# First MLP layer of token blocks 0 and 1 by seven products of halves for four of the seven chunk pairs, with the folded weights stored instead of kept in a buffer

## The chip, the core and the metric

The kernel runs on one core of one Trainium2 chip. A core has TensorE (PE), which multiplies matrices into PSUM banks; VectorE (DVE), ScalarE (ACT) and GpSimd (POOL), which do element-wise work; SyncE (SP), which here issues the transfers; and DMA engines, which carry them out. Every engine takes its own instructions in order, and semaphores order the engines against each other. The metric is the device time of one execution in microseconds (us).

## The reference

There are 2048 tokens of 640 features. The input is layernormed to `xn`, and the output is `x + attention(xn) + mlp(xn)`, where the MLP layernorms again:

```
x = A_x
xn = _layernorm(x, axis=-1)
return x + _A_ref(xn, A_wqkv, A_w_phi, A_wo) + _B_ref(xn, B_w1, B_b1, B_w2, B_b2)

# _B_ref: the MLP, 640 -> 1728 -> 640
y = _layernorm(x, axis=-1)
h = _gelu(jnp.einsum("bsd,df->bsf", y, w1) + b1)
return jnp.einsum("bsf,fd->bsd", h, w2) + b2

# _A_ref: linear attention, 32 heads of 20
pq = jnp.einsum("bhsd,hdf->bhsf", q, w_phi)
pk = jnp.einsum("bhsd,hdf->bhsf", k, w_phi)
phi_q = jnp.concatenate([_softmax(pq, axis=-1), _softmax(-pq, axis=-1)], axis=-1)
...
kv = jnp.einsum("bhsf,bhsd->bhfd", phi_k, v)
num = jnp.einsum("bhqf,bhfd->bhqd", phi_q, kv)
```

All operands are float32. `w_phi` follows the projections to q and k with nothing between, so the kernel multiplies it into their weights ahead of time; this product is called a fold.

## The kernel before, in words

**Exact products.** Every float32 operand is split into a high part, rounded to the type that PE takes in one pass (fp32r), and a low part, the rest. A product is then three matmuls, high by high, high by low and low by high (`mm3`, L61 to L64). Splitting is a copy on ACT (`hi`) and a subtraction on DVE or POOL (`lo`; both in `split`, L49 to L59). One group of three matmuls over 512 tokens is called a step below.

**Tiles.** Tokens come in four blocks of 512 (`b`). The 640 features are five k-chunks of 128 (`KC`). The 1728 hidden features are 14 chunks of 128 (the last has 64), worked on as seven pairs `g` = 0 to 6. The blocks 0 and 1 go through the MLP first, from about 18 to 130 us: this is the stage of the change. For a pair and a block, `Mlp.passes` (L258) does the first layer, 2 chunks x 5 k-chunks = 10 steps, with the GELU on ACT after each chunk (L251), and then the second layer, 5 output chunks x 2 = 10 steps, each output added to `acc[b]` by DVE (L300). The first layer of the next block or pair goes ahead of the second layer of the last, so that the GELU has time. PSUM banks 0 to 2 (`ph`) hold first layers, 5 to 7 (`po`) second layers, 3 and 4 (`px`) side work.

**Side work.** After every `mm3` of the first and second layers the generator `mlp.beside` is advanced by one (L247, L293); what it issues lands in the engines' queues at that place. In this stage it is `prep` (L567): the folds (`folds`), seven pairs of banks ten steps apart, products on PE (L510), highs on ACT (L528), lows on DVE (L530); the statistics of the tokens of blocks 2 and 3; then the row pairs: their means and scales are transposed on PE (L186), copied by DVE (L188), stored by SP (L189) and read back spread over all partitions (L193); the weights of v; and the layernormed tokens of blocks 2 and 3, on POOL (L603), DVE (L606), ACT (L610) and DVE (L613), stored for later (L615).

**Folds.** For each group of six heads the fold of k goes straight into the resident tile `wkv_` (wkh, wkl), that of q into a tile `t`, of which there are three, and from it to HBM in two stores (L533); the three narrow columns per head (18 of a group) go into `wkv_` too.

**Order.** PE's order is the order of the program text (L309), and so is that of DVE, ACT and POOL in this stage (L379). SP's order is chosen by a scheduler. A tile of a pool with n buffers waits for the readers of the tile n before it, transfers included.

## Time and profile before

| what | value |
|---|---|
| median of 3 runs | 712.67 us (711.66 to 712.88) |
| profiled execution, its own time | 713.22 us |
| span of its instructions | 711.3 us |
| mean granted TensorE clock | 1.000 |
| PE busy | 705.2 us, 99% of the span |
| DVE, ACT, POOL busy | 486.7, 334.4, 387.1 us |
| transfers | 98.25 MB, 138 GB/s on the mean |

"Busy" counts the time in which an engine has an instruction under way; register, branch and issue instructions don't count. In a list of groups a row has the line, engine, operation, output and inputs with shapes, the count, then busy time and mean nanoseconds of one, then the idle time of the engine ahead of the group and what ended it. In a timeline a row has start and duration in us, with the idle time ahead and its releaser in brackets. In the list of PE's waits a row has us in total, times and the longest. In a table by windows a row has the stretch, its length, busy time of PE, weight loads, DVE, ACT and POOL with counts, the granted clock, the share of the DMA engines and GB/s. PE's matmul rows overlap, since it is pipelined; the distance of their starts is what one costs.

### The profile page before, as it was taken

The numbers are of one execution on the slowest core, as the hardware profiler recorded it, in microseconds if no ns is written. First come the engines' busy times: TensorE is split into PE (matmuls) and PEld (weight loads), VectorE is DVE, ScalarE is ACT, GpSimd is POOL, SyncE is SP. The second block draws the span as 40 slices with busy tenths as digits, with TensorE's granted clock in tenths as the row PEclk, the third lists the DMA queues.
The fourth block names the chain that finished last, engine by engine and source line by source line (L and its number), as shares of the span: only waits on it lengthen the run. The fifth ranks groups of instructions, "written<-read, shape, count | busy, mean of one in ns | idle before, by whom it ended". The sixth has DMA issues, their size and how long they took to land.

```text
span 711.3 us, 9753 instructions
## 1 busy us (share of the span) xinstructions
PE 705.2 (99%) x3392; PEld 596.3 (84%) x3392; DVE 486.7 (68%) x827; ACT 334.4 (47%) x574; POOL 387.1 (54%) x339
## 2 busy tenths in 40 slices
PE   9999999999999999999999999999999999999998
PEld 7888888888888888888888888878888888888886
DVE  7837555875543798798788887745575656778653
ACT  7824355334213563464355458455565556551310
POOL 2011222465103896897787878556587777553400
PEclk9999999999999999999999999999999999999999
DMA  9714675454151313723600705774444653163222
GB/s 331 286 30 130 196 215 188 168 192 163 48 223 75 109 63 152 178 93 148 148 0 1 185 1 189 177 211 124 134 128 124 201 159 105 46 233 122 88 75 88
DMA packets 67924, 98.25 MB, mean 138 GB/s; under 512 B 14788, under 2 KB 37972, under 8 KB 66252
## 3 DMA queue, kind: packets, MB, share of 16 engines
q1 hardware_dynamic: 67876, 97.64, 43.4%
q8 instruction: 26, 0.43, 0.2%
q14 instruction: 22, 0.18, 0.1%
HBM read 67.27 MB, written 30.35 MB: 137 GB/s over the span
## 4 chain that ended last, share of the span: by engine, by line
PE 90%; issue 3%; DMA 2%; POOL 2%; DVE 2%; ACT 0%; SPq 0%; POOLq 0%; ACTq 0%
PE bank L62 27%; PE bank L64 26%; PE bank L63 26%; PE bank L748 2%; DMA r<-in_w 2%; PE bank L510 2%; PE bank L975 1%; PE bank L974 1%; POOL w L56 1%; PE bank L353 1%; PE bank L295 1%; PE bank L296 1%; PE bank L276 1%; PE bank L277 1%; DVE st L128 0%
## 5 line engine op out<-in xcount | busy, mean ns | idle before, releaser
L56 POOL TENSOR_TENSOR w<-r,w 128x640 fp32r<-128x640 f32 x48 | 77.7, 1639 | 111.5 <-ACT w L53 83.9
L62 PE MATMUL bank<-y,w 128*128 128x512 f32 (+1 forms) x310 | 120.3, 388 | 0.0
L64 PE MATMUL bank<-y,w 128*128 128x512 f32 (+1 forms) x310 | 119.9, 387 | 0.0
L63 PE MATMUL bank<-y,w 128*128 128x512 f32 (+1 forms) x310 | 119.8, 386 | 0.0
L62 PE MATMUL bank<-m,w 128*128 128x512 f32 x266 | 105.0, 395 | 0.2 <-DVE acc L300 0.2
L64 PE MATMUL bank<-m,w 128*128 128x512 f32 x266 | 103.6, 390 | 0.0
L63 PE MATMUL bank<-m,w 128*128 128x512 f32 x262 | 102.0, 389 | 0.0
L300 DVE TENSOR_TENSOR acc<-bank,acc 128x512 f32<-128x512 f32 x120 | 81.3, 683 | 27.9 <-PE bank L64 22.2
L62 PE MATMUL bank<-wkh,y 128*128 128x512 f32 (+2 forms) x240 | 87.6, 365 | 0.0
L63 PE MATMUL bank<-wkl,y 128*128 128x512 f32 (+2 forms) x240 | 87.1, 363 | 0.0
L64 PE MATMUL bank<-wkh,y 128*128 128x512 f32 (+2 forms) x240 | 86.9, 362 | 0.0
L64 PEld LDWEIGHTS bank<-y,w 128*128 128x128 f32 x310 | 58.2, 188 | 11.9
L63 PEld LDWEIGHTS bank<-y,w 128*128 128x128 f32 x310 | 58.3, 188 | 11.7
L62 PEld LDWEIGHTS bank<-y,w 128*128 128x128 f32 x310 | 58.2, 188 | 11.6
L713 POOL TENSOR_TENSOR m<-m,mx 128x640 f32<-128x640 f32 (+2 forms) x48 | 44.5, 941 | 42.8 <-DVE mx L701 42.8
L694 ACT ACTIVATE m<-bank 128x512 f32<-128x512 f32 (+1 forms) x64 | 26.5, 440 | 86.0 <-PE bank L64 62.6
L968 POOL TENSOR_TENSOR e<-e,m 128x512 fp32r<-128x512 f32 x28 | 40.0, 1430 | 39.4 <-ACT m L967 35.3
L62 PEld LDWEIGHTS bank<-m,w 128*128 128x128 f32 x266 | 50.0, 188 | 10.7 <-DVE acc L300 0.8
L64 PEld LDWEIGHTS bank<-m,w 128*128 128x128 f32 x266 | 49.9, 188 | 10.5
L720 DVE TENSOR_REDUCE sm<-m 128x64 f32<-128x1280 f32 x32 | 47.3, 1479 | 15.8 <-ACT m L718 15.6
L63 PEld LDWEIGHTS bank<-m,w 128*128 128x128 f32 x262 | 49.2, 188 | 9.6
L251 ACT ACTIVATE m<-bank,b1t 128x512 f32<-128x512 f32 (+1 forms) x54 | 36.2, 671 | 43.8 <-PE bank L64 42.8
(225 smaller groups left out, 1462.7 us busy)
## 6 DMA issues: line engine op xcount, KB each, us to landing
r<-in_w SPq DMA_DIRECT2D x52, 320.0 KB
e<-e SPq DMA_DIRECT2D x40, 256.0 KB
e<-acc SPq DMA_DIRECT2D x52, 160.0 KB
acc<-in_xT SPq DMA_DIRECT2D x4, 1280.0 KB
xb<-in_x SPq DMA_DIRECT2D x8, 320.0 KB
t<-in_x SPq DMA_DIRECT2D x8, 320.0 KB
raw<-in_xT SPq DMA_DIRECT2D x10, 256.0 KB
yh<-t SPq DMA_DIRECT2D x10, 256.0 KB
```

The costliest lines, as they stand in the source:

```text
L56: eng.tensor_tensor(lo, src, f(hi), op=ALU.subtract)
L62: nc.tensor.matmul(ps, lh, rh, start=first, stop=False, **kw)
L63: nc.tensor.matmul(ps, lh, rl, start=False, stop=False, **kw)
L64: nc.tensor.matmul(ps, ll, rh, start=False, stop=last, **kw)
L251: self.last = nc.scalar.activation(gt, pz, AF.Gelu_apprx_tanh, bias=b1t[:, 2 * g + j:2 * g + j + 1]).ins
L300: nc.vector.tensor_tensor(acc[b][:, m, :], pw, acc[b][:, m, :], op=ALU.add)
L510: nc.tensor.matmul(ps[:, c + i * kd:c + (i + 1) * kd], raw[n, g][:, (kc + i) * P:(kc + i + 1) * P], wpt[:, g, :kd // DF, 1:], start=True, ...
L694: return nc.scalar.activation(p3[:, :, c], ps.rearrange("p (h f) -> p h f", h=H), AF.Copy).ins
L713: subs[n, t] = nc.gpsimd.tensor_tensor(ep[:, s], a, b, op=ALU.subtract)
L720: nc.vector.tensor_reduce(sm, e.rearrange("p s (h f) -> p (s h) f", f=DH), axis=AX, op=ALU.add)
L748: nc.tensor.matmul(kvp[g // 2][:P, (g % 2) * 240:(g % 2) * 240 + 240].rearrange("p (s f) -> p s f", s=4), v[:, g * VS:g * VS + P], ft[:, : ...
L968: nc.gpsimd.tensor_tensor(pl, e, f(ph), op=ALU.subtract)
```

## The change

For the pairs `g` = 2 to 5 the first layer of both blocks is done together. The two chunks of hidden features, the two blocks, and the k-chunks 0-1 and 2-3 make a 2 by 2 by 2 product of halves, and this is done by seven products (each two steps) in place of eight, as Strassen and Winograd have it; the fifth k-chunk is done apart, in four steps of which two share an accumulation (operands 15, 25, 25 again, and the difference d5). That is 18 steps in place of 20. `cycle` (after) holds one pair: 18 steps of the first layer with the second layer of the last pair's block 1 between them, then ten steps of its own second layer for block 0, 38 in all. It needs

- four sums of tokens `t1` to `t4`, made once (`t_events`: two additions on POOL, four on DVE, highs on ACT, lows on DVE) from raw copies that ACT makes beside the split of y (`make_y01`);
- per pair four sums of weights S1 to S4 and a difference D5 on POOL, and highs (ACT) and lows (POOL) of ten operands, in place in the tiles w0 to w3 (`weight_events`);
- per pair four results: za, zb, zc come out of a running bank by copies on ACT (L732 of the changed kernel) while the bank goes on accumulating, and DVE adds other banks to them (`total`, L735); then GELU (L741), high (L742) and low (L746).

A list of events gives the step at which each is issued (`at_steps`); the side work of before runs beside it in the same steps (`both`). 

The folds no longer have a buffer of their own: `wkv_` is made only after the last cycle. Each group's fold, k or q, goes into a tile `t`, of which there are two, and to HBM in four stores (16 columns and 3 columns per head, high and low), and the folded weights of k and the narrow ones of q are read back at the end of the cycles. The first fold comes with cycle `g` = 2, where before it came with the first layer of pair 1, block 1. The row pairs and the tokens of blocks 2 and 3 now come ahead of the weights of v. In the attention's block 0 one partial tile is loaded with only the rows it has.

```diff
@@ Mlp @@
             yield
+            yield from self.second(g, b, hid, ws)
+
+        def second(self, g, b, hid, ws):
+
             for m in range(KC):
...
@@ main @@
+    def at_steps(*events):
+
+        n = 0
+        for when, what in sorted(events, key=lambda e: e[0]):
+            while n < when:
+                n += 1
+                yield
+            what()
+
...
+    ops = {"11": operand(0, 0, 2), "12": operand(0, 512, 2), "15": operand(0, 1024, 1), "s1": operand(1, 0, 2), "s2": operand(1, 512, 2),
+           "s3": operand(2, 0, 2), "22": operand(2, 512, 2), "25": operand(2, 1024, 1), "s4": operand(3, 0, 2), "d5": operand(3, 512, 1)}
+    s0, s1 = sraw[:, 0], sraw[:, 1]
+    (a11, a12, a15), (a21, a22, a25) = ([a[:, k] for k in (k1, k2, k5)] for a in araw)
+    raws_of = {"11": a11, "12": a12, "15": a15, "s1": s0, "s2": s1, "s3": s0, "22": a22, "25": a25, "s4": s0, "d5": s1[:, 0:1]}
+
...
+    def weight_events(times, step):
+
+        g = nc.gpsimd
+        events = [(times["S1"], add(g, s0, a21, ALU.add, a22)), (times["S1"] + 0.5, add(g, s1, s0, ALU.subtract, a11)),
+                  (times["S3"], add(g, s0, a11, ALU.subtract, a21)), (times["S4"], add(g, s0, a12, ALU.subtract, s1)),
+                  (times["D5"], add(g, s1[:, 0:1], a15, ALU.subtract, a25))]
+        for n, t in ops.items():
+            events += [(times[n], hi(t, raws_of[n])), (times[n] + 1, lo(t, raws_of[n], g))]
+        return events + [(max(times.values()) + 2, lambda: load_halves(step))]
+
+    def t_events():
+
+        (h0, l0), (h1, l1) = y[0], y[1]
+        v, g = nc.vector, nc.gpsimd
+        q1, q2, q3, q4 = traw
+        events = [(1, add(g, q1, f(h0[:, k1]), ALU.add, f(l0[:, k1]))), (3, add(g, q4, f(h0[:, k2]), ALU.add, f(l0[:, k2]))),
+                  (9, add(v, q1, q3, ALU.subtract, q1)), (11, add(v, q3, q2, ALU.subtract, q3)),
+                  (14, add(v, q2, q2, ALU.subtract, q1)), (16, add(v, q4, q4, ALU.subtract, q2))]
+        for i, when in ((0, 12), (2, 15), (1, 18), (3, 21)):
+            t = [thigh[i], tlow[i]]
+            events += [(when, hi(t, traw[i])), (when + 2, lo(t, traw[i], v))]
+        return events
+
...
@@ folds @@
-                    if kc == 0 and n == "k":
-                        dst[n, g] = [w[:, :, 96 * g:96 * g + 16 * nh] for w in wkv_]
-                    elif kc == 0:
-                        t = fp.tile([P, 2, KC, G5], F32R, name="t", bufs=3).rearrange("p a c f -> p a (c f)")[:, :, :KC * 16 * nh]
-                        dst[n, g] = [t[:, p].rearrange("p (c q) -> p c q", c=KC) for p in range(2)]
-                    c3, src = F1 + (F2 if n == "q" else 0) + 18 * g, srcs[:, i]
-                    main = [w[:, ks].rearrange("p c (h f) -> p c h f", f=16) for w in dst[n, g]]
-                    rest = [w[:, ks, c3:c3 + 3 * nh].rearrange("p c (h f) -> p c h f", f=3) for w in wkv_]
-                    both = [(*main, src[:, :, :, 0:16]), (*rest, src[:, :, :, 16:])]
+                    if kc == 0:
+                        dst[n, g] = fp.tile([P, 2, KC * G5], F32R, name="t", bufs=2)
+                    c3, src, ts = F1 + (F2 if n == "q" else 0) + 18 * g, srcs[:, i], dst[n, g]
+                    both = []
+                    for o, z in ((0, src[:, :, :, 0:16]), (16, src[:, :, :, 16:])):
+                        w = 3 if o else 16
+                        parts = [ts[:, p, o * KC * nh:(o + w) * KC * nh].rearrange("p (c q) -> p c q", c=KC) for p in range(2)]
+                        both.append((*(x[:, ks].rearrange("p c (h f) -> p c h f", f=w) for x in parts), z))
+                        if kc + ni == KC:
+                            dram = wq_dram if n == "q" and not o else wk_dram
+                            at = c3 if o else 96 * g
+                            stores += [(dram[p][:, :, at:at + w * nh], f(parts[p])) for p in range(2)]
                     for hi, _, z in both:
                         nc.scalar.activation(hi, z, AF.Copy)
                     for hi, lo, z in both:
                         nc.vector.tensor_tensor(lo, z, f(hi), op=ALU.subtract)
-                    if n == "q" and kc + ni == KC:
-                        for p in range(2):
-                            nc.sync.dma_start(wq_dram[p][:, :, 96 * g:96 * g + 16 * nh], f(dst[n, g][p]))
+            for to, t in stores:
+                nc.sync.dma_start(to, t)
 
...
@@ prep @@
         yield from rows(fp, mlp.px)
-        hi_lo = fp.tile([P, 2, KC, G5], F32R, name="t", bufs=3).rearrange("p a c f -> p a (c f)")
-        mrs = [row_pair(2, mtile(5).rearrange("p a t -> p (a t)")),
-               row_pair(3, fp.tile([P, 2, KC, G5], F32, name="t", bufs=3).rearrange("p a c f -> p (a c f)")[:, :8 * P])]
-
-        for kc in range(KC):
-            raw = next(loads)
-            for _ in range(3):
-                yield
-            split(*[w[:, kc, F1 + 2 * F2:] for w in wkv_], raw)
+        mrs = [row_pair(b, fp.tile([P, 2, KC * G5], F32, name="t", bufs=2).rearrange("p a c -> p (a c)")[:, :8 * P]) for b in range(2, 4)]
 
...
@@ main @@
+    def cycle(g, other, side):
+
+        (b11, b21, b51), (_, b22, b52) = ([[x[:, k] for x in y[b]] for k in (k1, k2, k5)] for b in range(2))
+        t1, t2, t3, t4 = zip(thigh, tlow)
+        bank, v, a = {}, nc.vector, nc.scalar
+        hid = [[mtile(i, F32R) for i in (1, 3)], [None, None]]
+        w2_ = [mlp.tiles[2 * (g % 2) + j][:, 2:4] for j in range(2)]
+
+        def product(ps, name, t, start=False):
+            s, n = ops[name], ops[name][0].shape[1]
+            for k in range(n):
+                mm3(bank[ps], s[0][:, k], s[1][:, k], t[0][:, k], t[1][:, k], start and k == 0, k == n - 1, skip_group_check=True)
+                next(mlp.beside, None)
+
+        def copy(z, ps):
+            return lambda: a.activation(z, bank[ps], AF.Copy)
+
+        def total(z, ps):
+            return lambda: v.tensor_tensor(z, bank[ps], z, op=ALU.add)
+
+        def gelu(b, j, z, ps=None):
+            def go():
+                if b:
+                    hid[b][j] = mtile(2 * j, F32R)
+                a.activation(z, bank[ps] if ps else z, AF.Gelu_apprx_tanh, bias=b1t[:, 2 * g + j:2 * g + j + 1])
+                a.activation(hid[b][j][:, 0, :512], z, AF.Copy)
+            return go
+
...
+        events = [(2, copy(za, "a")), (9, copy(zb, "a")), (14, total(za, "c")), (16, copy(zc, "a")), (16.5, total(zc, "d")),
+                  (17, gelu(0, 0, za)), (20, low(0, 0, za)), (21, gelu(0, 1, zd, "a")), (24, low(0, 1, zd)), (26, total(zb, "d")),
+                  (29, gelu(1, 1, zc)), (31, gelu(1, 0, zb)), (32, low(1, 1, zc)), (34, low(1, 0, zb)),
+                  (3, lambda: second_half(0)[0]()), (4, lambda: second_half(0)[1]()), (5, lambda: load_second(2 * g + 1)),
+                  (12, lambda: second_half(1)[0]()), (13, lambda: second_half(1)[1]())]
+        if g < 5:
+            events += [(14, lambda: load_second(2 * g + 2)),
+                       *weight_events({"11": 3, "S1": 4, "s1": 7, "s2": 10, "S3": 12, "12": 23, "15": 23, "s3": 24, "22": 25, "25": 25,
+                                       "S4": 26, "D5": 27, "s4": 28, "d5": 28}, g + 2)]
...
+        mlp.beside = both(at_steps(*((when - 1, what) for when, what in events)), side)
+        bank["a"] = mlp.ph()
+        product("a", "11", b11, True)
+        next(other)
+        bank["d"] = mlp.ph()
+        product("d", "s1", t1, True)
+        product("d", "25", b52)
+        product("a", "s2", t2)
+        next(other)
+        bank["c"] = mlp.ph()
+        product("c", "12", b21, True)
+        product("c", "15", b51)
+        product("a", "s3", t3)
+        next(other)
+        product("a", "22", t4)
+        product("a", "25", b51)
+        next(other)
+        product("d", "s4", b22)
+        product("d", "d5", b52)
+        next(other)
+        finish(other)
+        ws = [(None, None, w[:, 0], w[:, 1]) for w in w2_]
         for b in range(2):
+            parts = [(h[:, 0, :512], h[:, 1, :512]) for h in hid[b]]
             if b == 0:
...
+                finish(mlp.second(g, 0, parts, ws))
+        return mlp.second(g, 1, parts, ws)
+
+    before, side = p11, prep()
+    for g in range(2, 6):
+        before = cycle(g, before, side)
+    mlp.beside = side
+    ss.close()
```

Three places show how the order changes. Names carry buffer numbers; `t_...` are the fold tiles, `bank3` and `bank4` those of the folds.

ACT, the second pair of fold banks: before (copies of k's folds into wkh, and then a split of weights),

```order
L528 ACTIVATE wkh_617<-bank3_723 128x2x96
L528 ACTIVATE wkh_617<-bank3_723 128x2x18
L528 ACTIVATE wkh_617<-bank3_723 128x2x96
L528 ACTIVATE wkh_617<-bank3_723 128x2x18
L528 ACTIVATE wkh_617<-bank4_724 128x3x96
L528 ACTIVATE wkh_617<-bank4_724 128x3x18
L528 ACTIVATE wkh_617<-bank4_724 128x96
L528 ACTIVATE wkh_617<-bank4_724 128x18
L53 ACTIVATE w0_786<-r1_610 128x640
```

and now, in cycle 2 (m5_773 holds zc, bank0_776 is the running bank of that pair).

```order
L622 ACTIVATE t_832<-bank3_891 128x192
L622 ACTIVATE t_832<-bank3_891 128x36
L622 ACTIVATE t_909<-bank3_891 128x192
L622 ACTIVATE t_909<-bank3_891 128x36
L622 ACTIVATE t_909<-bank4_892 128x288
L622 ACTIVATE t_909<-bank4_892 128x54
L622 ACTIVATE t_931<-bank4_892 128x96
L622 ACTIVATE t_931<-bank4_892 128x18
L732 ACTIVATE m5_773<-bank0_776 128x512
```

Each group's copies now go to a tile, the third tile `t_931` follows two others, and the copy of zc stands right behind its two rows.

DVE, the last pair of fold banks: before (acc1 is the sum of block 1, wkl the resident low part),

```order
L530 TENSOR_TENSOR t_1095<-bank3_1144,t_1095 128x192
L530 TENSOR_TENSOR wkl_618<-bank3_1144,wkh_617 128x2x18
L530 TENSOR_TENSOR wkl_618<-bank3_1144,wkh_617 128x3x32
L530 TENSOR_TENSOR wkl_618<-bank3_1144,wkh_617 128x3x6
L530 TENSOR_TENSOR t_1165<-bank3_1144,t_1165 128x96
L530 TENSOR_TENSOR wkl_618<-bank3_1144,wkh_617 128x3x6
L530 TENSOR_TENSOR wkl_618<-bank4_1145,wkh_617 128x2x32
L530 TENSOR_TENSOR wkl_618<-bank4_1145,wkh_617 128x2x6
L530 TENSOR_TENSOR t_1165<-bank4_1145,t_1165 128x64
L530 TENSOR_TENSOR wkl_618<-bank4_1145,wkh_617 128x2x6
L56 TENSOR_TENSOR m1_1133<-m4_1132,m1_1133 128x512
L300 TENSOR_TENSOR acc1_100<-bank6_1208,acc1_100 128x512
```

and now, in cycle 3 (m4_772 holds zb, bank7_1390 is a second layer's bank).

```order
L624 TENSOR_TENSOR t_1303<-bank3_1354,t_1303 128x192
L624 TENSOR_TENSOR t_1303<-bank3_1354,t_1303 128x36
L624 TENSOR_TENSOR t_1369<-bank3_1354,t_1369 128x96
L624 TENSOR_TENSOR t_1369<-bank3_1354,t_1369 128x18
L624 TENSOR_TENSOR t_1374<-bank3_1354,t_1374 128x96
L624 TENSOR_TENSOR t_1374<-bank3_1354,t_1374 128x18
L735 TENSOR_TENSOR m4_772<-bank1_1174,m4_772 128x512
L624 TENSOR_TENSOR t_1369<-bank4_1355,t_1369 128x64
L624 TENSOR_TENSOR t_1369<-bank4_1355,t_1369 128x12
L624 TENSOR_TENSOR t_1374<-bank4_1355,t_1374 128x64
L624 TENSOR_TENSOR t_1374<-bank4_1355,t_1374 128x12
L310 TENSOR_TENSOR acc1_102<-bank7_1390,acc1_102 128x512
```

The total of zb and the addition that frees bank 7 now stand behind the lows of the tile `t_1374`.

POOL, from the first use of the row pair on: before (raw tiles less the rows of means, between weights' lows),

```order
L56 TENSOR_TENSOR w0_1268<-r1_1128,w0_1268 128x640
L56 TENSOR_TENSOR w0_1268<-r2_1129,w0_1268 128x640
L603 TENSOR_TENSOR raw_1309<-raw_1309,m5_1246 128x512
L603 TENSOR_TENSOR raw_1322<-raw_1322,m5_1246 128x512
L56 TENSOR_TENSOR w1_1383<-r1_1273,w1_1383 128x640
L56 TENSOR_TENSOR w1_1383<-r2_1274,w1_1383 128x640
L603 TENSOR_TENSOR raw_1338<-raw_1338,m5_1246 128x512
```

and now, at the start of cycle 4 (t_1483 is the row pair, sraw and a0, a1 the sums and raw weights of the next pair).

```order
L688 TENSOR_TENSOR raw_1278<-raw_1278,t_1483 128x512
L498 TENSOR_TENSOR w0_188<-r2_1263,w0_188 128x640
L501 TENSOR_TENSOR sraw_558<-a1_557 128x256
L498 TENSOR_TENSOR w0_188<-a0_556,w0_188 128x256
L501 TENSOR_TENSOR sraw_558<-sraw_558,a0_556 128x256
L498 TENSOR_TENSOR w1_189<-sraw_558,w1_189 128x256
L688 TENSOR_TENSOR raw_1358<-raw_1358,t_1483 128x512
L498 TENSOR_TENSOR w1_189<-sraw_558,w1_189 128x256
L501 TENSOR_TENSOR sraw_558<-a0_556,a1_557 128x256
L498 TENSOR_TENSOR w1_189<-r2_1513,w1_189 128x640
L688 TENSOR_TENSOR raw_1487<-raw_1487,t_1483 128x512
```

The subtraction with the row pair (L688) now stands ahead of the low of w0 and of the sums and lows of the next pair.

161 lines of the change are left out of this document (103 added, 58 removed).

## The prediction

> **What bounds the kernel now.** I read the busy times first, then what TensorE (PE) waited for, then the spacing of its matmuls in the stage that is changed, and last the helpers' queues around its folds.
>
> ```profile
> PE 705.2 (99%) x3392; PEld 596.3 (84%) x3392; DVE 486.7 (68%) x827; ACT 334.4 (47%) x574; POOL 387.1 (54%) x339
> PE 90%; issue 3%; DMA 2%; POOL 2%; DVE 2%; ACT 0%; SPq 0%; POOLq 0%; ACTq 0%
> ...
> PE bank L391 <- POOL m L389: 1.3, 1, 1.3
> PE bank L975 <- POOL e L968: 1.0, 2, 0.9
> PE bank L62 <- DVE acc L300: 0.2, 1, 0.2
> ```
>
> PE is busy for 705.2 of 711.3 us, makes up 90% of the chain of waits, and waits for other engines for 2.5 us in all. So a matmul taken away is time taken away, as long as no new wait fills its place; and every helper that comes late is paid in full, since PE has no slack of its own. The spacing of the matmuls, from the timeline of PE (start, duration):
>
> ```profile
> 34.54 0.39 PE L62 MATMUL bank<-y,w 128*128 128x512 f32 x1
> 41.37 0.39 PE L62 MATMUL bank<-m,w 128*128 128x512 f32 x1
> ```
>
> Between these two lie 30 matmuls back to back (the second layer's first one comes 30 after), so one takes 6.83/30 = 0.2277 us, and a step of three 0.683. The 0.39 is its passage, not its price.
>
> **What is removed.** Per pair of chunks and both blocks the first layer had 4 x 5 x 3 = 60 matmuls. Seven products of two k-chunks and three products of the fifth chunk beside the d5 one make 18 steps, 54 matmuls. Six fewer in each of four pairs are 24, and the PE order of the change has 24 fewer 128x512 matmuls: the rival that a scheduler undoes it falls away. The gain is 24 x 0.2277 = **5.46 us**, in this stage and nowhere else. The folds of the weights have the same passes on PE before and after, 1.77 us for 16 of them.
>
> **What is added under cover.** The busy time of each engine in two stretches of the stage (PE, weight loads, DVE, ACT, POOL):
>
> ```profile
> 61.80:92.50 30.70, 30.70 (x161) 26.29 (x160) 19.25 (x55) 13.09 (x34) 9.54 (x6) 1.00 0.61 185
> 92.50:123.00 30.50, 30.50 (x152) 25.67 (x151) 17.51 (x43) 15.85 (x36) 6.78 (x4) 1.00 0.65 195
> ...
> L300 DVE TENSOR_TENSOR acc<-bank,acc 128x512 f32<-128x512 f32 x120 | 81.3, 683 | 27.9 <-PE bank L64 22.2 <-PE bank L296 3.6
> L56 POOL TENSOR_TENSOR w<-r,w 128x640 fp32r<-128x640 f32 x48 | 77.7, 1639 | 111.5 <-ACT w L53 83.9 <-issue 27.6
> L1127 POOL TENSOR_TENSOR wos<-woc 128x256 f32<-128x256 f32 x4 | 3.4, 853 | 0.0
> L1127 POOL TENSOR_TENSOR wos<-wos,woc 128x256 f32<-128x256 f32 x2 | 1.9, 934 | 0.2
> L1124 POOL TENSOR_TENSOR e<-wos,e 128x256 fp32r<-128x256 f32 x5 | 3.9, 794 | 12.8 <-ACT e L1121 12.7
> L1121 ACT ACTIVATE e<-wos 128x256 fp32r<-128x256 f32 x5 | 2.0, 410 | 4.5 <-POOL wos L1127 4.5
> L53 ACT ACTIVATE y<-bank 128x512 fp32r<-128x512 f32 x4 | 2.4, 588 | 1.3 <-PE bank L171 1.2
> ```
>
> A cycle of 38 steps lasts 26 us on PE. It gives POOL five sums (0.85) and ten lows (0.79 at most) for two lows of 1.64: 4.3 + 7.9 - 3.3 = 8.9 more. ACT gets ten copies of 0.41 and three of 0.59, 5.9 more; DVE three totals of 0.68, 2.0 more. On top of what the rows show for 30 us, POOL comes to at most 19, ACT to 22, DVE to 22 of 30: no engine becomes the bound by its sum, and I cost these at nothing beside PE. Without that cover one late bank copy would cost its 0.59. The 36 more stores go by SP, which computes nothing. The folded weights are read back once, 2 x 128 x 5 x 704 x 4 bytes = 3.6 MB, after the last cycle, at the 389 GB/s of a row below some 9.3 us, beneath 130 matmuls (30 us) that don't need them: nothing, and some microseconds at most if they came that late.
>
> What isn't covered is order. ACT, DVE and POOL take their rows in a fixed order, and three rows now wait for a transfer with PE's work queued behind them.
>
> **Place 1, the second fold pair of cycle 2.** ACT's first copy for k3 needs the tile that k1 had (two buffers, was three), so it waits until k1's four stores have landed; behind it stands the copy of zc out of its bank, which PE needs at step 19. From the chain of waits, and from the timelines of ACT and SP:
>
> ```profile
> 76.23 1.78 PE bank L510 x16
> 102.09 1.52 PE bank L510 x14
> ...
> 77.15 0.33 ACT L528 ACTIVATE wkh<-bank 128x96 fp32r<-128x96 f32 x2 [2.08 <-PE bank L510]
> 83.56 0.33 ACT L528 ACTIVATE t<-bank 128x192 fp32r<-128x192 f32 x1 [4.83 <-DMA wql<-t]
> ...
> 77.16 0.86 SPq L480 DMA_DIRECT2D raw<-in_wqT  x2
> 78.66 0.65 SPq L533 DMA_DIRECT2D wqh<-t  x1
> 79.40 0.59 SPq L533 DMA_DIRECT2D wql<-t  x1
> ...
> L533 SPq DMA_DIRECT2D wqh<-t x6: 518/526/652, 78.7 to 106.1; - x6
> ```
>
> Counted from the fold's start: the first bank is ready at 77.15 - 76.23 = 0.92, k1's copy ends at 1.25. Four issues of 0.53, with gaps of about 0.08 as between the two at 78.66 and 79.40, end at 3.7. The landing behind the last issue, L, is the unknown. The existing store was issued by 79.99 and let ACT go on at 83.56: 3.57 us. But reads stood ahead of it:
>
> ```profile
> 81.00:82.00 1.00, 1.00 (x7) 0.81 (x6) 0.00 (x0) 0.00 (x0) 0.00 (x0) 1.00 1.15 324
> 82.00:83.00 1.00, 1.00 (x6) 0.84 (x5) 0.00 (x0) 0.00 (x0) 0.00 (x0) 1.00 0.42 115
> 83.00:84.00 1.00, 1.00 (x6) 0.84 (x5) 0.00 (x0) 0.45 (x3) 0.00 (x0) 1.00 0.00 0
> ```
>
> The DMA engines run until about 82.4 and then stop, so the landing itself took 83.56 - 82.4 = 1.15, and the rest was two reads of 320 KB and the second store's own bytes. A store of four bytes times 16 x 128, row L189 below, was followed 1.03 after its issue by the load that waits for it. In the change 572 KB go out in 2.4 us of issues, which 324 GB/s just keeps up with, so I take L = 1.15 and keep 1.03 and 3.57 as bounds. Then ACT has 0.25 + 0.18 for k3's copies and 0.59 for zc: 3.7 + 1.15 + 1.02 = 5.87. PE comes to step 19 at 1.77 + 0.08 + 5 x 0.683 = 5.27. **Stall 0.6** (0.5 to 3.0).
>
> The Trainium skill, "DMA: Bandwidth & Descriptors", section "Anatomy of one DMA", puts a fixed 2.0 us on a transfer, mostly the receipt of the write, and most when it goes to HBM. The 1.15 and 1.03 here are about half of it. By the page L would be 2.0, the stalls of places 1 and 2 would grow by 0.85 each, and the time would be 714.1.
>
> **Place 2, the last fold of cycle 3.** The same with q5 behind q4: first bank 1.15 into the fold (estimated from the 0.92), copy to 1.5, four issues to 4.0, landed at 5.15. ACT's copy 0.25, then DVE's lows, in its order:
>
> ```profile
> L530 DVE TENSOR_TENSOR t<-bank,t 128x96 fp32r<-128x96 f32 x3 | 0.8, 254 | 0.8 <-ACT wkh L528 0.8
> L530 DVE TENSOR_TENSOR t<-bank,t 128x64 fp32r<-128x64 f32 x1 | 0.2, 224 | 0.4 <-ACT wkh L528 0.4
> L530 DVE TENSOR_TENSOR wkl<-bank,wkh 128x18 fp32r<-128x18 f32 x7 | 1.2, 166 | 0.0
> ```
>
> 0.25 + 0.17, the total of zb 0.68, two lows of 0.22 and two of about 0.16, and the addition that frees the bank 0.68: 2.55. Together 5.15 + 0.25 + 2.55 = 7.95, where PE wants the bank at 1.52 + 0.08 + 7 x 0.683 = 6.4. **Stall 1.55** (1.4 to 4.0).
>
> **Place 3, the start of cycle 4.** The row pairs of blocks 2 and 3 go PE, DVE, SP, HBM and back, and POOL's first y product waits for them with the weight sums of the next pair queued behind it. From the timelines, and by windows:
>
> ```profile
> 113.05 0.27 PE L186 MATMUL bank<-idt,sc 128*16 128x128 f32 x1
> 113.66 0.34 SPq L189 DMA_DIRECT2D r<-sr  x1
> 115.03 0.33 SPq L193 DMA_DIRECT2D m<-r  x1
> 116.00:118.00 2.00, 2.00 (x11) 1.65 (x10) 1.18 (x2) 0.79 (x2) 2.00 (x2) 1.00 0.86 238
> 118.00:120.00 2.00, 2.00 (x11) 1.65 (x9) 0.00 (x0) 1.13 (x2) 1.30 (x1) 1.00 1.01 389
> L603 POOL TENSOR_TENSOR raw<-raw,m 128x512 f32<-128x512 f32 x5 | 6.8, 1377 | 4.7 <-DMA raw<-in_xT 4.7
> L610 ACT ACTIVATE t<-raw 128x512 fp32r<-128x512 f32 x10 | 6.3, 628 | 15.7 <-DVE raw L606 15.7
> L606 DVE TENSOR_TENSOR raw<-raw,t 128x512 f32<-128x512 f32 x5 | 4.2, 834 | 0.0
> ```
>
> The first pair's 512 KB are in about 118.2, 5.15 after the transpose. Before, nothing due on PE stood behind POOL there. Now the transpose runs after step 1 of the cycle, at 0.68, and POOL goes on at 5.83: product 1.38, low of the second layer's weights 1.64, S1 0.85, ACT's high 0.41 and, behind it on ACT, the copy of zb 0.59: 10.70. PE wants it at 0.3 + 14 x 0.683 = 9.86: stall 0.84. From S1's end at 9.70: two lows 1.58, S2 0.93, the second product 1.38, DVE 0.83, ACT 0.63, and then the copy of zc 0.59: 15.64, where PE is ready at 10.70 + 4 x 0.683 = 13.43: stall 2.2. **Together 3.0.** With POOL's small operations at 256/640 of 1.64 = 0.66 and the pair landing 0.35 sooner it is 2.0; with it landing 1.15 after its last byte, as above, 4.2.
>
> **Sum.** 0.6 + 1.55 + 3.0 = 5.15 given back of 5.46. The profiled execution took 713.22 us, 0.55 above the median of the runs, 1.9 around the span; the differences apply to both, so from the median 712.67 - 0.3 = **712.4 us**. With all bounds together the given-back time is 3.9 to 11.2.
>
> **Rivals.**
> 1. No wait shows, full gain: 712.67 - 5.46 = 707.2. For it, PE hardly waits anywhere now; against it, three rows in the order wait for transfers that take longer than PE's way there. It would need a row pair within 2.2 us of its transpose, where 5.15 are shown. Chance 0.10.
> 2. Part of the waits: without place 3 (POOL catches up) 709.4, without places 1 and 2 (the stores land as PE arrives) 710.2. Chance 0.24, since each stall is a difference of two numbers of 5 to 15 us.
> 3. Slower: the stores land late because reads stand ahead of them. SP's order has a 320 KB read just ahead of k1's stores, and their runs of 72 bytes, which the trace of before lacks, can drain slower than its runs of 384. Every microsecond of L costs two, one in each place: from L = 2.0 it is slower by over 0.2%, at 2.8 it is 715.7, at the 3.57 of the trace 717.2. Against it, the store of that row had twice the reads ahead. Chance 0.23.
> 4. A wait so long that PE itself starts slowly again. At the start of the kernel:
>
> ```profile
> 1.30:4.70 3.40, 3.39 (x8) 2.71 (x9) 0.97 (x3) 0.92 (x2) 0.00 (x0) 1.00 0.83 264
> ```
>
> 8 matmuls in 3.40 us are 0.425 each instead of 0.228, at a granted clock that reads 1.00; once more would cost 3.4 x (1 - 0.228/0.425) = 1.6 us, 714.0, and 715.6 for two. The longest wait I find is 2.2 us, after which no row here shows it. Chance 0.05. The Trainium skill, "TensorE: Matmul & The Clock Gate", Part 1, has half clock after about 3.4 us of idleness and as long to come back; no run here shows that after a wait.
>
> **How the numbers follow.** The forecast keeps 0.38. A measurement of this kernel tells about 0.2%, 1.43 us, from no change. Its own range is 711.1 (L = 1.03 and place 3 at 2.0) to 713.9 (L = 1.9, two places times 0.75 more), within that. Faster holds rivals 1 and 2, 0.34; slower holds rivals 3 and 4, 0.28, the latter since a wait that long comes on top of the others. Same is the forecast's 0.38. The range of 708.4 to 716.2 leaves out the full gain and the landings above L = 3.0, together some 0.2.
>
> **What would show it.** PE loses 24 matmuls and its span in the stage from 18 to 130 us changes little; new PE waits stand behind ACT's copies (L732) near the second fold pair of cycle 2 and in cycle 4, and behind DVE's additions (L310) near the last fold. ACT at k3's first copy (L622) would name a DMA of wkl as its releaser, POOL's L688 the DMA of the rows. The forecast is wrong if PE's waits in the stage sum to under 3.7 or over 6.9 us, and its mechanism is wrong if they stand elsewhere.

## The result and the profile after

The changed kernel takes 747.59 us (median of 4 runs, 745.66 to 748.15) against 712.6 us of the kernel before: a ratio of 1.0485, 95% interval 1.0472 to 1.0498. It is slower by 35 us. The forecast was 712.4 us with a range to 716.2, so the sign, the size and the range were all missed.

The page of the changed kernel, its first part, the row of the granted clock, the chain by engine and by line:

```profile
PE 714.9 (96%) x3368; PEld 599.7 (80%) x3368; DVE 510.5 (68%) x847; ACT 353.7 (47%) x626; POOL 421.8 (57%) x393
PEclk9999899899999999999999999999999999999999
PE 79%; DMA 7%; issue 5%; DVE 4%; POOL 3%; ACT 2%; SPq 0%; ACTq 0%; POOLq 0%; DVEq 0%
...
DMA packets 92791, 105.39 MB, mean 141 GB/s; under 512 B 38420, under 2 KB 61604, under 8 KB 91116
```

PE has 3368 instructions, 24 fewer than before, as the change says. Yet it is busy for 714.9 us, 9.7 longer, and idle for 31.3 instead of 6.1. Transfers, which made up 2% of the chain before, make up 7%, and there are 38420 packets under 512 bytes where the page of before has 14788.

PE's waits (us in total, times, longest):

```profile
PE bank L62 <- DVE acc L310: 16.0, 6, 6.5
PE bank L62 <- ACT m L732: 9.2, 4, 5.9
```

and the windows in which the wait stands and those right after it, for four of the six places where the clock changed (length, then busy time of PE, weight loads, DVE, ACT, POOL, the granted clock, the DMA share, GB/s):

```profile
46.73:50.14 3.41, 0.94 (x4) 0.48 (x3) 3.38 (x4) 2.20 (x5) 0.85 (x3) 1.00 0.00 0
50.14:53.55 3.41, 3.41 (x9) 2.63 (x8) 3.41 (x4) 1.74 (x3) 3.41 (x3) 0.50 0.00 0
84.28:87.69 3.41, 0.00 (x0) 0.00 (x0) 0.00 (x0) 0.00 (x0) 0.00 (x0) 1.00 1.15 170
87.69:91.10 3.41, 1.32 (x3) 1.13 (x4) 1.68 (x5) 2.05 (x5) 0.00 (x0) 0.50 0.94 143
91.10:94.52 3.42, 3.42 (x9) 2.65 (x9) 2.51 (x7) 0.50 (x1) 0.00 (x0) 0.50 0.74 174
...
159.37:162.78 3.41, 1.31 (x6) 0.81 (x5) 3.31 (x4) 1.49 (x3) 3.41 (x4) 1.00 0.10 35
162.78:166.19 3.41, 3.41 (x9) 2.63 (x9) 1.45 (x2) 1.15 (x2) 3.41 (x5) 0.50 0.73 214
...
210.57:213.98 3.41, 1.26 (x6) 0.72 (x6) 3.39 (x6) 1.29 (x3) 1.81 (x2) 1.00 0.69 160
213.98:217.39 3.41, 3.41 (x9) 2.64 (x10) 3.41 (x7) 0.00 (x0) 0.00 (x0) 0.50 1.01 391
```

A window of 3.41 us in which PE was busy for 1.3 us or less is followed by one or two at half clock (the granted clock reads 0.50). What a matmul costs there, from the timeline of PE:

```profile
50.59 0.63 PE L64 MATMUL bank<-m,w 128*128 128x512 f32 x1
53.15 0.58 PE L64 MATMUL bank<-m,w 128*128 128x512 f32 x1
```

The second is the sixth after the first, so one starts every 0.427 us where it was 0.2277, and 47% of the busy time of such a window is lost. There are nine of them before 220 us, with 26.1 us of busy PE in them, which cost 12.2 us. The whole account, by place (waits from the timeline of PE, of which the four longest are shown; of the half-clock windows behind a place 47% of their busy time):

```profile
49.82 0.54 PE L62 MATMUL bank<-m,w 128*128 128x512 f32 x1 [2.47 <-DVE acc L310]
...
89.78 0.80 PE L62 MATMUL bank<-th,w 128*128 128x512 f32 x1 [5.86 <-ACT m L732]
...
143.94 0.79 PE L62 MATMUL bank<-m,w 128*128 128x512 f32 x1 [6.46 <-DVE acc L310]
...
184.11 0.80 PE L62 MATMUL bank<-m,w 128*128 128x512 f32 x1 [2.98 <-DVE acc L310]
```

| place | wait of PE, us | half clock, us |
|---|---|---|
| token sums, 30.6 to 49.8 | 0.5 + 0.8 + 2.5 | 1.6 |
| second fold pair of cycle 2, 89.8 (place 1) | 5.9 | 2.2 |
| cycle 3, 126.0 | 0.6 | - |
| last fold, 143.9 (place 2) | 6.5 | 2.4 |
| row pair, 162.5 and 167.7 (place 3) | 2.1 + 0.6 | 1.6 |
| end of cycle 4, 178.1 and 184.1 | 0.5 + 3.0 | 2.8 |
| weights of the last chunk, 213.9 and 229.7 | 2.2 + 1.4 | 1.6 |

That is 26.6 + 12.2 = 38.8 us. The span grew by 746.2 - 711.3 = 34.9, and with the 5.5 us of the products 40.4 have been lost: the table holds them but for 1.6. The list counts a wait from the end of the matmul before, 0.39 us after its start, while the next could have started after 0.23; 0.16 for each of the twelve waits is 1.9, about the rest. The places follow one by one below. The read-back of the folded weights, costed at nothing, has no wait of PE behind it.

The wait of place 1, from the timelines of ACT and SP:

```profile
79.63 0.42 ACT L622 ACTIVATE t<-bank 128x192 fp32r<-128x192 f32 x2 [2.07 <-PE bank L599]
88.91 0.33 ACT L622 ACTIVATE t<-bank 128x96 fp32r<-128x96 f32 x2 [7.44 <-DMA wkl<-t]
89.12 0.60 ACT L732 ACTIVATE m<-bank 128x512 f32<-128x512 f32 x1
...
79.99 1.22 SPq L626 DMA_DIRECT2D wkh<-t  x2
81.30 1.56 SPq L626 DMA_DIRECT2D wkl<-t  x2
...
84.00:88.00 4.00, 0.00 (x0) 0.00 (x0) 0.00 (x0) 0.00 (x0) 0.00 (x0) 0.96 1.22 163
```

The row, the releaser and the copy of zc behind it (L732) are those that the prediction named. Four stores are issued from 79.99 to 82.86, and ACT goes on at 88.91: L (the time from the last issue to the landing) is 6.05 us, where 1.15 was taken and 3.57 was the upper bound. For four microseconds no engine does anything, while the DMA engines are at work all the time (share 1.22) and move 163 GB/s. In the window of before shown in the prediction a share of 1.15 went with 324 GB/s.

### The profile page after: what moved, and what is told of

Read it like the earlier page. It is cut to its first block, busy times and chain, and to the rows that moved or that the text cites. A ratio compares the mean times of both kernels' runs of the same rounds, so it can differ in the third digit from the quotient of the medians.

```text
span 746.2 us, 9972 instructions
## 1 busy us (share of the span) xinstructions
PE 714.9 (96%) x3368; PEld 599.7 (80%) x3368; DVE 510.5 (68%) x847; ACT 353.7 (47%) x626; POOL 421.8 (57%) x393
## 2 busy tenths in 40 slices
DMA packets 92791, 105.39 MB, mean 141 GB/s; under 512 B 38420, under 2 KB 61604, under 8 KB 91116
## 4 chain that ended last, share of the span: by engine, by line
PE 79%; DMA 7%; issue 5%; DVE 4%; POOL 3%; ACT 2%; SPq 0%; ACTq 0%; POOLq 0%; DVEq 0%
PE bank L62 24%; PE bank L63 23%; PE bank L64 23%; DMA wkl<-t 4%; PE bank L927 2%; DMA r<-in_w 2%; PE bank L1156 1%; PE bank L1155 1%; DMA xb<-in_x 1%; DVE acc L310 1%; DVE t L624 1%; POOL w L56 1%; DVE q L501 1%; PE bank L305 1%; ACT t L622 1%
## 5 line engine op out<-in xcount | busy, mean ns | idle before, releaser
L62 PE MATMUL bank<-m,w 128*128 128x512 f32 x266 | 109.1, 410 | 16.8 <-DVE acc L310 16.0
L64 PE MATMUL bank<-m,w 128*128 128x512 f32 x266 | 106.4, 400 | 0.0
L63 PE MATMUL bank<-m,w 128*128 128x512 f32 x262 | 105.4, 402 | 0.0
L62 PE MATMUL bank<-y,w 128*128 128x512 f32 (+1 forms) x270 | 105.4, 390 | 0.0
L64 PE MATMUL bank<-y,w 128*128 128x512 f32 (+1 forms) x270 | 105.0, 389 | 0.0
L63 PE MATMUL bank<-y,w 128*128 128x512 f32 (+1 forms) x270 | 105.0, 389 | 0.0
L62 PEld LDWEIGHTS bank<-m,w 128*128 128x128 f32 x266 | 52.2, 196 | 30.7 <-DVE acc L310 18.8
L56 POOL TENSOR_TENSOR w<-r,w 128x640 fp32r<-128x640 f32 x31 | 48.6, 1584 | 28.5 <-ACT w L53 27.5
L64 PEld LDWEIGHTS bank<-m,w 128*128 128x128 f32 x266 | 52.0, 196 | 11.5
L1149 POOL TENSOR_TENSOR e<-e,m 128x512 fp32r<-128x512 f32 (+1 forms) x28 | 39.5, 1410 | 38.3 <-ACT m L1148 34.2
L64 PEld LDWEIGHTS bank<-y,w 128*128 128x128 f32 x270 | 51.1, 189 | 10.5
L62 PEld LDWEIGHTS bank<-y,w 128*128 128x128 f32 x270 | 51.2, 189 | 10.4
L63 PEld LDWEIGHTS bank<-y,w 128*128 128x128 f32 x270 | 51.2, 189 | 10.3
L63 PEld LDWEIGHTS bank<-m,w 128*128 128x128 f32 x262 | 51.2, 195 | 10.2
L897 ACT ACTIVATE m<-m,rs_all 128x1280 f32<-128x1280 f32 x32 | 43.8, 1368 | 21.9 <-POOL m L892 21.9
```

What stands on the lines that cost most here:

```text
L56: eng.tensor_tensor(lo, src, f(hi), op=ALU.subtract)
L62: nc.tensor.matmul(ps, lh, rh, start=first, stop=False, **kw)
L63: nc.tensor.matmul(ps, lh, rl, start=False, stop=False, **kw)
L64: nc.tensor.matmul(ps, ll, rh, start=False, stop=last, **kw)
L897: exps[n, t] = nc.scalar.activation(e, e, AF.Exp, scale=rs_all[:, t:t + 1])
L1149: nc.gpsimd.tensor_tensor(pl, e, f(ph), op=ALU.subtract)
```

## The experiments

Theory S: a fold tile's reuse waits for stores that land late in a DMA queue filled by short runs, and each wait that empties a window costs half clock on top. Theory O: the orders of the helpers' queues cost the time, and the stores are only named last. Four small places (token sums, row pair, end of cycle 4, last chunk) should be cured by order alone. The expectations count a half-clock window as half of its busy time, 1.7 us for a full one, where the account above has 1.6. The kernels named e1, e2, e3, e5 and e6 are one edit each to the changed kernel.

**Four fold tiles** (e1_four_tiles):

```diff
-                        dst[n, g] = fp.tile([P, 2, KC * G5], F32R, name="t", bufs=2)
+                        i4, turns[0] = turns[0] % 4, turns[0] + 1
+                        dst[n, g] = (fp.tile([P, 2, KC * G5], F32R, name="t", bufs=2) if i4 < 2
+                                     else ap.tile([P, 2, KC * G5], F32R, name=f"t{i4}"))
```

> The changed kernel with four fold tiles in place of two (the third and fourth lie in the space beside the raw weights, which is free until the read-back). Theory S (a fold tile's reuse waits for stores that land late in a full DMA queue, and PE's waits of over 2 us halve its clock for one or two stretches of 3.41 us after them): the waits of 5.9 us at 89.8, 0.6 at 126.0 and 6.5 at 143.9 go, and with them two stretches of 6.83 us at half clock, of which some 4.9 us of busy PE each cost half: 13.0 + 4.9 = 17.9 less, about 730 us. Rival O (the waits come from the order of the helpers' queues, the stores are only the last to be named): the waits stay, over 742 us. Rival Q (the DMA queue is too full for the work, whatever the ring): the wait moves to the loads of the raw weights and the folds on PE themselves wait, over 738 us.

Measured: 733.22 us, ratio 1.0289 (1.0263 to 1.0315), 14.4 less than the change. The waits at 89.8, 126.0 and 143.9 are gone. But one of 7.4 us stands at the row pair, where 2.1 were. From the timelines of SP and POOL of this kernel:

```profile
136.57 0.38 SPq L192 DMA_DIRECT2D r<-sr  x1
140.75 0.81 SPq L196 DMA_DIRECT2D t<-r  x2
...
144.96 1.26 POOL L690 TENSOR_TENSOR raw<-raw,t 128x512 f32<-128x512 f32 x1 [16.04 <-DMA t<-r]
```

The 8 KB store of the rows lands 3.8 us after its issue, where the trace of before shows 1.03, and POOL starts 8.4 us after the store's issue. So O falls for the folds, and Q is right in part: with more tiles the queue is as full as it was, and the next small transfer that somebody waits for pays.

**Narrow columns kept on the chip** (e2_thin_kept): they go into a buffer of 128x5x192 and are stored once, in runs of 768 bytes.

```diff
-                        parts = [ts[:, p, o * KC * nh:(o + w) * KC * nh].rearrange("p (c q) -> p c q", c=KC) for p in range(2)]
+                        if o:
+                            parts = [x[:, :, c3 - F1:c3 - F1 + 3 * nh] for x in thin]
+                        else:
+                            parts = [ts[:, p, 0:16 * KC * nh].rearrange("p (c q) -> p c q", c=KC) for p in range(2)]
-                        if kc + ni == KC:
+                        if kc + ni == KC and not o:
```

> The changed kernel with two fold tiles, but the narrow columns (3 per head) kept in a buffer on the chip and stored once at the end, so that each tile has two stores in place of four and no run of 72 bytes. Theory S: what fills the DMA queue is the count of short runs (12800 of 72 bytes take 10.8 us of the 16 engines, 12800 of 384 bytes 22.5), so a third of that goes, the landing comes some 2 to 3 us sooner and each of the two long waits shrinks to about 3; 747.6 - 2 x 3 - 2 x 1.7 = about 738 us. Rival O: no change, 746 to 748.

Measured: 738.86 us, ratio 1.0369 (1.0332 to 1.0405), as S expected. In its profiled execution the two long waits are 2.3 and 4.0 us, where they were 5.9 and 6.5.

**Token sums four steps later** (e3_sums_later):

```diff
-                  (9, add(v, q1, q3, ALU.subtract, q1)), (11, add(v, q3, q2, ALU.subtract, q3)),
-                  (14, add(v, q2, q2, ALU.subtract, q1)), (16, add(v, q4, q4, ALU.subtract, q2))]
+                  (13, add(v, q1, q3, ALU.subtract, q1)), (15, add(v, q3, q2, ALU.subtract, q3)),
+                  (18, add(v, q2, q2, ALU.subtract, q1)), (20, add(v, q4, q4, ALU.subtract, q2))]
```

(their highs and lows four later too)

> The changed kernel with DVE's and ACT's part of the token sums four steps later, POOL's two additions where they are. Theory C (DVE's first difference stands ahead of an addition that frees a bank, waits for POOL's sum, and runs 3.4 us because POOL works at the same time, where the second one runs 1.2): the wait of 2.5 us at 49.8 goes, and the 3.41 us at half clock after it: 1.7 less, together 4.2, about 743.4 us. Rival: the sums are then late for cycle 2, and the wait only moves there, 747 or more.

Measured: 742.36 us, ratio 1.0414 (1.0397 to 1.0432), 5.2 less than the change. It isn't the clean case that was expected: the wait of 2.5 us became two, of 1.0 at 49.8 and 1.7 at 64.0, the second just ahead of cycle 2, where the lows of the sums now stand in front of DVE's additions: in part the wait only moved, as the rival had it. Neither halves the clock, so 1.6 us of half clock are gone; the wait of place 1 is 4.6 us here and has one half-clock window less behind it, which is part of the 5.2.

**The stores alone** (e4_stores_alone): the kernel before, without products, but with two fold tiles, four stores each and the read-back.

```diff
-                    if kc == 0 and n == "k":
-                        dst[n, g] = [w[:, :, 96 * g:96 * g + 16 * nh] for w in wkv_]
-                    elif kc == 0:
...
+                    if kc == 0:
+                        dst[n, g] = fp.tile([P, 2, KC * G5], F32R, name="tf", bufs=2)
...
+                            stores += [(dram[p][:, :, at:at + w * nh], f(parts[p])) for p in range(2)]
...
+            for to, t in stores:
+                nc.sync.dma_start(to, t)
```

> The kernel before with only the folds changed: no resident buffer for them, two tiles, four stores each, read back at the last pair; no products of halves, and the order of before. Theory S in its strong form (the stores are what costs, with or without the products): ACT's copies wait for tiles and hold up the GELU behind them, 3 to 15 us slower than before, 716 to 728 us. Rival T (the waits cost only where a bank copy of the products stands right behind them, since the GELU of before has slack): within 2 us of before, 711 to 714.5.

Measured: 730.28 us, ratio 1.0247 (1.0232 to 1.0263), 17.8 slower than before and more than the 15 at the upper end of what S expected. T falls. PE's waits and ACT's:

```profile
PE bank L62 <- DVE acc L301: 6.2, 3, 4.7
PE bank L62 <- DVE acc L299: 4.2, 1, 4.2
ACT tf L534 <- DMA wkl<-tf: 24.1, 5, 6.6
```

The GELUs and additions behind ACT's copies have no slack for 6.6 us either. So the stores alone, without any product, cost half of what the change lost.

**Row pair used ten steps later** (e5_rows_later):

```diff
+        for _ in range(10):
+            yield
         for i, (b, c) in enumerate(todo):
```

> The changed kernel with the tokens of blocks 2 and 3 begun ten steps (6.8 us) later, so that POOL's first product with the row pair no longer stands ahead of the weights' sums while the pair is under way. Theory S plus place 3 of the prediction (POOL, blocked by the pair, is late for the copies of zb and zc): the waits of 2.1 and 0.6 us at 162.5 and 167.7 go, and the stretch of 3.41 us at half clock: 1.7 less, together 4.4, about 743 us; and if POOL's lateness is also what delays the chain at 178 to 184, these 0.5 and 3.0 us and 6.83 us at half clock go too, another 6.4, about 737. Rival O (POOL has more than a cycle's work in cycle 4 wherever the product stands): the waits come back some steps later, 746 or more.

Measured: 740.48 us, ratio 1.0399 (1.037 to 1.0428). The waits at the row pair are gone, the end of cycle 4 keeps 1.2 and 0.5 of its 3.5 without half clock. But 1.5 and 0.6 us are new at the end of cycle 5, where the delayed work now is, and the last chunk's waits grow to 3.1 and 2.1, with a half-clock window each. The waits of places 1 and 2, which the edit doesn't touch, are 4.2 and 5.5 here, where they were 5.9 and 6.5: some 2.6 of the 7.1 us gained are theirs.

**The last chunk's weights on POOL** (e6_last_on_pool): `split`, fill and cast of chunk 13 with `nc.gpsimd` in place of `nc.vector`.

> The changed kernel with the weights of the last chunk (lows, fills and the cast) on POOL in place of DVE, which has them ahead of the additions that free the banks. Theory D: the waits of 2.15 us at 213.9 and 1.4 at 229.7 go, with 3.41 us at half clock: 2.15 + 1.44 + 1.7 = 5.3 less, about 742.3. Rival: POOL, shared by other work, is then late for these weights and PE waits at the last pair, 746 or more.

Measured: 738.18 us, ratio 1.0359 (1.0342 to 1.0377). The 2.15 us are gone and 0.4 of the 1.4 stay. It gained 9.4 us, more than the 5.3 expected: earlier waits moved too (the one of place 1 is 4.7), and three of its places have one half-clock window fewer, so about 4 us of the difference don't belong to this edit.

**All of them** (e7_all), with the sums spread a little otherwise and ACT's raw copies a step later:

> All the cures in one: four fold tiles, narrow columns kept on the chip and stored once, token sums spread over the steps in which DVE has less to do (and ACT's raw copies a step later), the row pair's use ten steps later, the last chunk's weights on POOL. Theory S with its four smaller places accounts for the whole difference (26.7 us of waits, some 13 us at half clock, less the 5.5 of the products): with all of them gone it must come out near 712.6 - 5.5 = 707, 706.5 to 710. Rival Q (products and stores together want more of the DMA queue or of POOL than there is): waits remain, 714 to 725.

Measured: 720.41 us, ratio 1.0112 (1.0097 to 1.0128): 27.2 of the 35 us are back, but not the 38 or more that were expected. No wait at a fold is left. Of what is left 3.9 us and one half-clock window belong to the token sums, 3.3 to additions behind a y product that waits for POOL, and 2.1 to v's weights. The cause at the sums, from the timeline of DVE, two differences of the same size:

```profile
43.56 3.40 DVE L502 TENSOR_TENSOR q<-q,q 128x1024 f32<-128x1024 f32 x1 [2.29 <-POOL q L502]
51.39 1.26 DVE L502 TENSOR_TENSOR q<-q,q 128x1024 f32<-128x1024 f32 x1
...
40.69 5.19 POOL L502 TENSOR_TENSOR q<-y,y 128x1024 f32<-128x1024 f32 x2
```

The first runs beside the second of POOL's two additions and takes 3.40 us, the later one 1.26.

**Tuned in turn** (e8_tuned): the additions of the token sums on DVE (and the steps of the sums moved, not shown), the subtraction of the means on DVE, the lows of v on POOL.

```diff
-        events = [(1, add(g, q1, f(h0[:, k1]), ALU.add, f(l0[:, k1]))), (3, add(g, q4, f(h0[:, k2]), ALU.add, f(l0[:, k2]))),
+        events = [(1, add(v, q1, f(h0[:, k1]), ALU.add, f(l0[:, k1]))), (3, add(v, q4, f(h0[:, k2]), ALU.add, f(l0[:, k2]))),
...
-            nc.gpsimd.tensor_tensor(xc, xc, mr[:, 0], op=ALU.subtract)
+            nc.vector.tensor_tensor(xc, xc, mr[:, 0], op=ALU.subtract)
...
-            split(*[w[:, kc, F1 + 2 * F2:] for w in wkv_], raw)
+            split(*[w[:, kc, F1 + 2 * F2:] for w in wkv_], raw, eng=nc.gpsimd)
```

> As e7_all, with what its trace left cured in turn: the two additions of the token sums on DVE, which is idle when they are due, so that POOL and DVE no longer work at once there (2.7 us of waits at 47.6 and 64.2, and 3.41 us at half clock); the subtraction of the row of means on DVE in place of POOL (1.6 us at 157.7 to 159.8, 1.6 at 187.6); the lows of v's weights on POOL (2.1 at 212.9). Theory: e7_all's 720.4 less 1.2 + 2.7 + 1.7 + 1.6 + 1.6 + 2.1 = 709.5, and at best 707.2, since no other wait is in its trace: 706.5 to 711, faster than the kernel before. Rival: work moved onto DVE only shifts the waits to its additions, 713 to 721.

Measured: 714.41 us, ratio 1.0024 (1.0015 to 1.0033), short of the expectation again. One wait of 3.1 us is new, at 51.2: the highs of the sums had been put ahead of a GELU in ACT's queue and wait there for DVE.

**The last two waits** (e9_best): those highs behind the GELUs, one addition later, and the highs of S4 and D5 (which wait for POOL) behind the GELUs that end a cycle.

```diff
...
-                                       "S4": 26, "D5": 27, "s4": 28, "d5": 28}, g + 2)]
+                                       "S4": 26, "D5": 27, "s4": 31.5, "d5": 31.5}, g + 2, 30)]
```

> As e8_tuned, with the two waits its trace still has cured: of the token sums only one addition before the steps in which DVE adds (the other after them), and the copies of their highs behind the GELU on ACT, which they held up (3.1 us at 51.2); and the highs of S4 and D5, which wait for POOL, behind the GELUs at the end of a cycle (0.6 at 156.2). Theory: e8_tuned's 714.4 less 3.1 + 0.6 = 710.7, and between 709 and 711.5; faster than the kernel before by 0.2 to 0.4%. Rival: the sums are late for cycle 2 then, or only shift the wait, 713 or more.

Measured: 710.09 us against 712.65 of before, ratio 0.9961 (0.9947 to 0.9975): faster than before by 0.4%, half of what the 24 matmuls are worth. The page and the waits of this kernel:

```profile
PE 699.5 (99%) x3368; PEld 591.1 (83%) x3368; DVE 511.6 (72%) x844; ACT 353.3 (50%) x626; POOL 423.4 (60%) x396
...
PE bank L62 <- DVE acc L308: 1.5, 2, 1.1
PE bank L1165 <- DVE acc L1176: 1.2, 1, 1.2
PE bank L358 <- DVE xb L163: 1.0, 1, 1.0
PE bank L62 <- DVE acc L310: 0.8, 1, 0.8
```

PE is busy 5.7 us less than before, which is the 5.46 that the prediction worked out for the products, and the waits of 4.5 us listed here, where before had 1.2 beside the 1.3 that both have, keep 3.3 of it. Only 2.3 us of these waits lie in the stage of the change (at 33.7, 61.1 and 179.9); the 1.0 stands at 7.9 us and the 1.2 at 572.7, and their cause is open.

**The change's stores put back into that kernel** (e10_stores_as_changed): e9_best without the four tiles and the kept columns.

> e9_best with the change's own way with the folds put back: two tiles, four stores each, runs of 72 bytes among them. Theory S: the stores are now the only cause left, and their waits come back with their stretches at half clock: 12 to 14 us of waits at the folds and 3 to 5 us of half clock, and some at the row pair, 724 to 732 us, about half of the change's whole loss. Rival O (order was the cause, and with the orders cured the stores have slack to land in): within 3 us of e9_best.

Measured: 724.32 us, ratio 1.0167 (1.015 to 1.0183): the stores cost 14.2 us by themselves, with every order cured. ACT's wait and PE's:

```profile
ACT t L622 <- DMA wkl<-t: 18.9, 4, 6.7
PE bank L62 <- ACT m L734: 5.1, 1, 5.1
```

**Each half of the cure taken out** (e11_two_tiles: e9_best with two tiles; e12_thin_stored: e9_best with the narrow columns stored in 72-byte runs).

> e9_best with two fold tiles in place of four; the narrow columns stay on the chip. It tells the ring from the short runs: if the wait for a tile is what costs, with two stores of 384-byte runs per tile in a queue that has room, each of the two waits is about that of e2_thin_kept (2.3 and 4.0 us) with one stretch at half clock or two: 715 to 719 us. If the short runs alone filled the queue, 710 to 712.

> e9_best with the narrow columns stored piece by piece as in the change (72-byte runs), but four fold tiles. If the ring is what costs, within 2 us of e9_best, 710 to 712. If the queue is too full, the wait comes at the row pair as in e1_four_tiles (7.4 us there, of which the ten steps, 6.8 us, may hide nearly all) and in the loads behind SP: 713 to 720.

Measured: 718.78 us (ratio 1.0101, 1.0082 to 1.012) with two tiles, 715.44 (1.0048, 1.0033 to 1.0063) with the short runs. The ring of two costs 8.7, the short runs 5.3, together 14.0 of the 14.2: both halves of the cure are needed, and within the intervals their costs add up. The waits with two tiles are 2.8 and 4.5 us at places 1 and 2; with the short runs there is one, of 3.6 at 144.9, near the row pair's place, where ACT waits for a load of weights ahead of the copy of zc:

```profile
143.67 0.74 ACT L495 ACTIVATE w<-r 128x640 fp32r<-128x640 f32 x1 [4.48 <-DMA r<-in_w]
```

## Why the prediction was wrong, step by step

Three steps failed: the landing L at places 1 and 2 (stalls of 2.15 us forecast, 12.3 measured), the places that were costed at nothing (10.9 us of waits), and the clock, which was kept out of the sum with a chance of 0.05 (12.2 us). By the prediction's own sign its mechanism holds for 15.7 of the 26.6 us of waits, those at the folds and the row pair, and is wrong for the other 10.9, which stand elsewhere.

**The gain was right.** 24 fewer matmuls, 5.46 us; e9_best has PE busy 5.7 us less. The part under cover was right for the sums of the engines (none became the bound in a cycle), and the read-back was hidden.

**Places 1 and 2: right mechanism, wrong size.** The step that failed here is the landing L. It was worked out as 1.15 us on the ground that 572 KB in 2.4 us of issues "324 GB/s just keeps up with". That prices bytes. In the records of the changed kernel's transfers a run of 72 bytes holds a DMA engine for 13.5 ns on the mean, one of 384 for 28 and one of 2560 for 132, so a byte in the shortest runs costs 3.6 times as much as in the longest. The share of the DMA engines at places 1 and 2 (1.15 and 0.89 in the windows of 84.28 and 138.89) is that of a full queue at half the rate (170 and 143 GB/s), and fewer short runs brought time back (8.7 us in e2, 5.3 from e12 to e9). How much of the full queue is due to the reads that stand ahead of the stores was not separated. L was 6.05 at place 1; the rest of the 5.3 us that the stall was short of is in the issues, which took 2.87 us where 2.45 were counted. At place 2 the chain has two such waits in a row, where the prediction had counted one (ACT waited 3.0 us for the tile ahead of it, and then 5.1):

```profile
135.73 0.33 ACT L622 ACTIVATE t<-bank 128x96 fp32r<-128x96 f32 x2 [3.04 <-DMA wkl<-t]
141.12 0.52 ACT L622 ACTIVATE t<-bank 128x96 fp32r<-128x96 f32 x4 [5.06 <-DMA wkl<-t]
```

The stalls came to 5.9 and 6.5 us for 0.6 and 1.55. Rival 3 was this case, with the right reason against the forecast (short runs drain slower, reads stand ahead); but its price stopped at the 3.57 of a row in which two stores were under way, and its chance was 0.23. The prediction quoted that store's own landing of 3.57 and then argued it down. Taken as it stood, it would have given 717.2, still 30 us short.

The Trainium skill, "DMA: Bandwidth & Descriptors", section "Anatomy of one DMA", has a fixed 2.0 us, which it fitted to transfers that GpSimd issues; here SP issues them. The traces have 1.03 and 1.15 in a queue with room (before) and 3.8 (e1) to 6.05 (after) in a full one: what was missing was the queue, not the fixed part.

**Place 3: the right mechanism, and luck in the size.** 3.0 was forecast, 2.7 measured, on the operations that were named: POOL's product behind the row pair, then the copies of zb and zc.

```profile
157.57 1.29 POOL L688 TENSOR_TENSOR raw<-raw,t 128x512 f32<-128x512 f32 x1 [13.09 <-DMA t<-r]
...
162.51 0.59 PE L62 MATMUL bank<-th,w 128*128 128x512 f32 x1 [2.10 <-ACT m L732]
167.72 0.50 PE L62 MATMUL bank<-th,w 128*128 128x512 f32 x1 [0.60 <-ACT m L732]
```

But the parts are wrong: 0.84 was forecast for zb, and it was 2.1, since POOL went on 6.3 us after the transpose (at 151.26) and not 5.15. For zc 2.2 was forecast, and it was 0.6, since the half clock after the first wait had held up PE itself by some 1.6 us. The two errors cancel in the sum. e5 took both waits away by moving that product.

**Rival 4, the clock, was priced at one or two events and at 0.05.** It happened six times, and cost 12.2 us. The reason given against it was wrong, that no row shows it after a wait of 2.2 us: a wait of 2.1 us did it at 162.5. The windows above show what it takes in this kernel, a window in which PE is busy for 1.3 us or less, and then one or two follow at half clock.

**What was not seen.** Three places were costed at nothing "beside PE" by the sums of an engine over a cycle: token sums (5.4 us with the half clock behind them), the end of cycle 4 (6.3) and the last chunk (5.2). There a short wait of a helper's queue met an addition or a GELU behind it. The prediction said itself that what isn't covered is order, and then went through the order at three places only. e5 to e9 removed most of these waits by moving operations between engines or behind others, with the same work to do, which shows that order and the choice of engine were the cause. e7 to e9 hold several such moves each, so what a single one is worth isn't shown there.

So in place of the 5.15 us given back by the sum, some 40 were: 15.7 of waits at the folds and the row pair (5.9, 0.6, 6.5 and 2.7), 10.9 of waits at places that had been passed over, 12.2 of half clock, and the small rest of the table. What stays open is what a full queue costs by itself when nobody waits at a tile: e12's 5.3 us come from one late load and the half clock after it, and might be cured by an earlier load, which wasn't tried.

## What to carry to other kernels

Price a store by its number of runs and by how full the queue is when it goes out, not by its bytes alone; and when a buffer is given up so that its content goes through memory, count the tiles in flight against the landing of a full queue, here 4 to 6 us for 0.3 to 0.6 us of copies. On an engine that never waits, go through every helper's queue in its fixed order at each new event; sums over a cycle hide the waits that count. A saving in matmuls can be had, but only after the waits are out: the same products came with a loss of 35 us as they were first put in, and with a gain of 2.6 us in e9_best.
